# Three output parts together in the first block's second product, and a sparser chain of maxima

## The chip, the cores and the metric

The kernel runs on one core of a Trainium2 chip, as one launch. The metric is the device time of that launch in microseconds (us), the median of three runs. Engines are named PE (TensorE), DVE (VectorE), ACT (ScalarE), POOL (GpSimd) and SP (SyncE, which here only issues DMAs).

## The reference: what is computed

```python
# q, k, v: (4, 8, 768, 64): 4 batches, 8 heads, 768 tokens
k_sum = k.reshape(B, H, nb, 32, D).max(axis=3)      # 24 blocks of 32 keys
v_sum = v.reshape(B, H, nb, 32, D).mean(axis=3)
scores_l = scale * q @ k^T, kept where |i - j| < 16, else -1e9
scores_s = scale * q @ k_sum^T + log(32)
a = softmax(concat[scores_l, scores_s])             # sum + 1e-9
attn = a @ concat[v, v_sum]
# x = attn as (3072, 512); 4 experts, w1 (4, 512, 1024), w2 (4, 1024, 512)
p = domain_probs / (domain_probs.sum(-1) + 1e-9)
out = sum over e of p[:, e] * (relu(x @ w1[e]) @ w2[e])
```

All is float32. The kernel keeps the precision by splitting an operand into a high and a low part and adding three products of them.

## The kernel before, in words

**Tiling.** The 3072 tokens are 8 blocks of 384 (`TB`). A block's attention is 8 pieces (96 queries, 4 heads each). A piece loads keys and values, splits them on ACT and POOL (`stage_a`), makes scores on PE, maxima on DVE and exponentials on ACT (`scores`), normalises and splits the probabilities (`probs`), turns them by a DMA (`transposed`, tile awT), multiplies with the values on PE (`values`, tile px) and writes the block's x (`to_x`).

**The passes.** The first block is passed over alone with experts 0 and 1, the second alone with 1 and 0, then both together with 2 and 3. Blocks 2 to 7 go as three pairs with all four experts, in the order 2, 3, 1, 0 (`plan`, `pair_units`). A pass of one expert has a first product (tiles ph; in pairs pha, phb, phc, phd, by a scheme of seven products for eight) and a second one (tiles po, functions `second` and `mm2`). `mm2(tb, e, ts, hT, w2)` runs the output parts `ts` (a part is 128 tokens) through the eight chunks of w2: for each chunk and part three matmuls of 512 columns. So one part is 24 matmuls. It holds one bank of PSUM for each part from its first matmul until DVE has added the part to the sum (tile acc). There are four banks for ph and po (`ps_mm`), two for scores and two, `ps_av`, which px, the bank phd of pairs, and both tiles of the chain below share. `second` runs the last block of a pass as part 0 alone and then parts 1 and 2 together, before the change.

**The chain that spreads maxima.** In pairs the operands are 16 bit wide, after scaling by powers of two, found from the largest weights (tiles w0 to w3) and values (v1 to v3). `spread_maxima` brings a column of 128 maxima to one and back to all partitions, in four steps: 0, PE turns the column (tile w3t for expert 3); 1, DVE takes the maximum, limits and masks it and copies it out over 128 columns (tile w3e); 2, PE multiplies it with a piece of the identity (tile w3s); 3, DVE copies it back and `scales` works out factors (tile found). One call does at most one step. Steps wait on `passed`, a count of matmul time that the calling loops add up (2.1 us for a unit of a plain first product, 1.05 us for one of a pair's 28 products, 1.39 or 2.08 us for a unit of a second product). In a pair's first product the chain is only called after the 6th and the 7th of each seven products, so once or twice in 7.35 us. Seven chains run in all, one after another.

**What sets the order.** Instructions up to the first attention of block 0 are pinned to program order. Behind that a planner orders each engine's instructions by their place in the program and a timeline of its own; at run time every engine works through its list in order. Attention steps are put between units of the products, by the share of the pass that is done (`advance`). `prepare` scales the experts' weights on ACT and DVE, a step at a time; its 22nd, 42nd and 62nd steps are the first that need the factors of experts 3, 1 and 0.

Of the kernel before, what the change touches and what calls it, by code (L numbers as in the profile page):

```python
# [66 lines left out]
def attn_moe(ctx: ExitStack, tc: tile.TileContext, qvL, qv0, v0L, kD, kT, vT, w1L, w2L, dpL, cst, out):  # L67
# [60 lines left out]
    def facts(k):  # L128
        taken[0] += k
        return found[:, taken[0] - k : taken[0]]  # L130
# [9 lines left out]
    pending, last_matmul, passed = [], [None], [0.0]  # L140
    chain = dict(stage=0, due=0.0)

    def spread_maxima():

        if chain["stage"] == 0:
            if not pending:
                return
            chain["t"] = t = pending.pop(0)
            k = t["k"]
            t["turned"] = ps_av.tile([P, 512], F32, name=f"{t['name']}t", tag="av")[:k, 0:P]  # L150
            PE.transpose(t["turned"], t["m"], ident)
            chain.update(stage=1, due=passed[0] + 1.5)
            return
        if passed[0] < chain["due"]:
            return
        t = chain["t"]
        k = t["k"]
        if chain["stage"] == 1:
            most = facts(1)[:k]
            V.tensor_reduce(most, t["turned"], axis=AX.X, op=ALU.max)  # L160
            V.tensor_scalar(most, most, LEAST, MOST, op0=ALU.max, op1=ALU.min)
            bits = most.bitcast(I32)
            V.tensor_single_scalar(bits, bits, 0x7F800000, op=ALU.bitwise_and)
            t["every"] = sb.tile([P, P], F32, name=f"{t['name']}e", tag="hs", bufs=2)[:k]
            V.tensor_copy(t["every"], most.broadcast_to([k, P]))
            chain.update(stage=2, due=passed[0] + 3.0)
        elif chain["stage"] == 2:
            t["spread"] = ps_av.tile([P, 512], F32, name=f"{t['name']}s", tag="av")[:, 0:k]
            PE.matmul(t["spread"], t["every"], ident[:k, :k], start=True, stop=True)
            chain.update(stage=3, due=passed[0] + 1.5)  # L170
        else:
            V.tensor_copy(t["m"], t["spread"])
            t["then"](*scales(t["m"], k))
            chain["stage"] = 0

    def scales(m, k):

        both = facts(2 * k)
        s, inv = both[:, 0:k], both[:, k : 2 * k]
        V.tensor_scalar_mul(inv, m, 1.0 / TOP)  # L180
        V.tensor_scalar(s.bitcast(I32), m.bitcast(I32), -1.0, float(0x7F000000), op0=ALU.mult, op1=ALU.add)
        V.tensor_scalar_mul(s, s, TOP)
        return s, inv
# [855 lines left out]
    def mm2_halves(tb, e, t, hT, w2):  # L1039
        gt = tb * (TB // P) + t  # L1040
        pe = pw[:, gt, e : e + 1]
        for c in range(2):
            cols = slice(c * DM // 2, (c + 1) * DM // 2)
            po = ps_mm.tile([P, 512], F32, name=f"po{tb}_{e}_{t}{c}", tag="mm")[:, 0 : DM // 2]
            for m, (fc, (whi, wlo)) in enumerate(w2.items()):
                hh, hl = (x[:, t * P : (t + 1) * P] for x in hT[tb, fc])
                PE.matmul(po, hh, whi[:, cols], start=m == 0, stop=False)
                PE.matmul(po, hh, wlo[:, cols], start=False, stop=False)
                PE.matmul(po, hl, whi[:, cols], start=False, stop=m == FC - 1)
            V.scalar_tensor_tensor(acc[gt][:, cols], po, pe, acc[gt][:, cols], op0=ALU.mult, op1=ALU.add)  # L1050
            SP.dma_start(out[gt * P : (gt + 1) * P, cols], acc[gt][:, cols])
            yield 3 * FC * US2 / 2, 1.0

    def mm2(tb, e, ts, hT, w2):
        po = {t: ps_mm.tile([P, 512], F32, name=f"po{tb}_{e}_{t}", tag="mm") for t in ts}
        done = 0
        for m, (fc, (whi, wlo)) in enumerate(w2.items()):
            for t in ts:
                hh, hl = (x[:, t * P : (t + 1) * P] for x in hT[tb, fc])
                PE.matmul(po[t], hh, whi, start=m == 0, stop=False)  # L1060
                PE.matmul(po[t], hh, wlo, start=False, stop=False)
                last_matmul[0] = PE.matmul(po[t], hl, whi, start=False, stop=m == FC - 1)
                done += 3 * US2
            if m < FC - 1 and (len(ts) > 1 or m in (2, 5)):
                yield done, 1.0
                done = 0
        for t in ts:
            gt = tb * (TB // P) + t
            pe = pw[:, gt, e : e + 1]
            added[gt] = added.get(gt, 0) + 1  # L1070
            if added[gt] == 1:
                acc[gt] = sb.tile([P, DM], F32, name=f"acc{gt}", tag="acc", bufs=6)
                V.tensor_scalar_mul(acc[gt], po[t], pe)
            else:
                V.scalar_tensor_tensor(acc[gt], po[t], pe, acc[gt], op0=ALU.mult, op1=ALU.add)
            if added[gt] == E:
                SP.dma_start(out[gt * P : (gt + 1) * P, :], acc.pop(gt))
        yield done, 1.0
# [8 lines left out]
    def second(tbs, e, hT, w2, last):  # L1087
        whole = tbs if last else tbs[:-1]
        for tb in whole:
            for t in range(TB // P):  # L1090
                ends = last and (tb, t) == (tbs[-1], TB // P - 1)
                yield from mm2_halves(tb, e, t, hT, w2) if ends else mm2(tb, e, [t], hT, w2)
        for tb in tbs[len(whole) :]:
            yield from mm2(tb, e, [0], hT, w2)
            yield from mm2(tb, e, [1, 2], hT, w2)

    def with_steps(units, pr, e, w2):
        plain, final = pr is None, pr is not None and e == PAIRS[0][1][-1]
        if plain:
            steps = LATE if e == plan[2][1][-1] else ()  # L1100
        else:
            steps = SECOND if pr == SCALED else ()
        for n, us in enumerate(units):
            if plain and e in PLAIN:
                if 3 <= n < 3 + FC:
                    scan_w2(e, n - 3, w2[n - 3])
                if n == 3 + FC:
                    maxima_of(e)
                passed[0] += us[0]
                spread_maxima()  # L1110
            if not plain:
                passed[0] += us[0]
                spread_maxima()
                if pr == SCALED and n % 4 != 3:
                    next(looks.get(e, iter(())), None)
            if n in steps:
                next(preparing, None)
            if (pr, e) == FIRST7 and n in LAST2:
                next(preparing_last, None)
            soon = (12, 15) if (pr, e) in SEVENTH else (13, 17)  # L1120
            if final and pr < PAIRS[-1][0] and n in soon:
                fetch_parts(pr + 1, PAIRS[pr][1][0], soon.index(n))
            yield us

    def plain_units(tbs, e, early=0):
# [24 lines left out]
        for fc in order:  # L1150
            if fc not in w1:
                w1[fc] = weights(w1L, e, fc, "1", PL)
            for tb in tbs:
                us = mm1(fc, tb, w1[fc], KC // 2 if fc < early else 0)
                if e in PLAIN:
                    if tb == tbs[0]:
                        scan_plain(e, fc, w1[fc])
                    passed[0] += us[0]
                    spread_maxima()
                yield us  # L1160
            if fc not in w2:
                w2[fc] = weights(w2L, e, fc, "2", V if len(tbs) == 1 else PL)
        kept[e] = {fc: w1[fc] for fc in order[-4:]}, w2
        yield from with_steps(second(tbs, e, hT, w2, False), None, e, w2)


# [127 lines left out]
    def pair_units(pr, e, last=False):  # L1294
# [70 lines left out]
        if final:  # L1365
            yield from with_steps(seven_second(pr, tbs, e, hop), pr, e, {})
            return
        w2 = {fc: half2.pop((pr, e, fc)) for fc in range(FC)}
        yield from with_steps(second(tbs, e, hT, w2, last), pr, e, w2)


# [46 lines left out]
    for (tbs, experts), end in zip(plan, ENDS):  # L1418
# [11 lines left out]
        parts, due, u, done = None, [], 0.0, 0.0  # L1430
        for e, k in zip(experts, ease):
# [4 lines left out]
            for us, pace in units:  # L1436
# [4 lines left out]
                if nxt < NTB // 2 and u > whole - seconds[-1] + 1e-3:  # L1441
                    if parts is None:
                        xpair[nxt], parts = x_operands(nxt)
                    if due and u > due[0][0]:
                        due.pop(0)[1]()
                        due = [(max(t, u + XGAP), f) for t, f in due]
# [69 lines left out]
```

## Time and profile before

| | |
|---|---|
| three runs | 1138.64, 1131.49, 1139.86 us; median 1138.64 |
| the profiled execution | 1133.09 us, span 1131.3 us |
| granted TensorE clock, mean | 0.989 |
| PE / DVE / ACT / POOL busy | 1090.1 / 790.1 / 688.1 / 605.2 us |

The profiled execution has its own time beside its span: 1.8 us lie around the span. All rows below are of that execution, and times in them count from the span's start. A timeline row is start, duration, engine, line, operation, output <- inputs, count, and in brackets the idle time of the engine before it with what ended it. All engines' rows carry line 79, since one helper issues every instruction; tiles tell them apart.

### The profile page before, as it was taken

The page shows a single profiled execution, that of the slowest core. Times are in us where ns is not written, and L with a number is a line of the kernel's source. Part 1 is how long each engine was busy: PE and PEld are TensorE (multiplying, and loading weights), DVE is VectorE, ACT ScalarE, POOL GpSimd, SP SyncE. Part 2 cuts the span into 40 slices and gives each one's busy share as a digit, 9 for nine tenths or more (in the row PEclk, how much of TensorE's full clock was granted, in tenths as well). Part 3 has the DMA queues.
Part 4 walks back from the last instruction along what each step waited for, and adds up shares of the span by engine and source line. Part 5 has one row for each costly group of instructions (what it writes and reads, how often), then busy time and mean ns, then how long its engine had stood idle before and what let it go on. Part 6 is the DMA issues. An engine that isn't in the chain of part 4 may idle for free. (4 is left out here: it accounts for less than half of the span.)

```text
span 1131.3 us, 22766 instructions
## 1 busy us (share of the span) xinstructions
PE 1090.1 (96%) x7857; PEld 783.8 (69%) x7857; DVE 790.1 (70%) x1910; ACT 688.1 (61%) x1863; POOL 605.2 (53%) x722
## 2 busy tenths in 40 slices
PE   9898799999999899899999999999999999999998
PEld 7778688898898655555556455555586868686867
DVE  6668576568877986867888666666756875656573
ACT  5577476666597668777668455655636563636361
POOL 2298377785676645444274425444546664546451
PEclk9998989999999999999999999999999999999999
DMA  6598559667766788969899766564635482626201
GB/s 248 197 264 233 148 153 297 162 191 177 217 184 187 229 253 261 296 180 326 251 282 274 245 212 150 132 163 104 189 92 183 156 257 68 201 62 209 66 20 56
DMA packets 205027, 214.12 MB, mean 189 GB/s; under 512 B 82289, under 2 KB 140145, under 8 KB 204913
## 3 DMA queue, kind: packets, MB, share of 16 engines
q1 hardware_dynamic: 204912, 212.68, 64.3%
q8 instruction: 61, 1.00, 0.4%
q14 instruction: 54, 0.43, 0.1%
HBM read 157.45 MB, written 38.27 MB: 173 GB/s over the span
## 5 line engine op out<-in xcount | busy, mean ns | idle before, releaser
L79 POOL TENSOR_TENSOR ks<-kr,ks 128x304 fp32r<-128x304 f32 x112 | 101.4, 911 | 137.5 <-ACT ks L79 125.1
L79 PE MATMUL po<-w,hh 128*128 128x512 f32 x384 | 122.6, 399 | 0.0
L79 ACT ACTIVATE ms<-ms,nb 96x152 f32<-96x152 f32 x256 | 104.4, 415 | 19.0 <-DVE nb L79 18.4
L79 PE MATMUL po<-w2s,hh 128*128 128x512 f16 x384 | 114.8, 380 | 0.0
L79 PEld LDWEIGHTS <-wls 128*128 128x128 f16 x768 | 74.5, 98 | 48.7 <-issue 1.0
L79 PE MATMUL ph<-xh,wh 128*128 128x384 f32 x256 | 89.6, 354 | 9.1 <-ACT wh L79 5.6
L79 PEld LDWEIGHTS <-hh 128*128 128x128 f16 x576 | 53.3, 98 | 58.5
L79 PEld LDWEIGHTS <-hws 128*128 128x128 f16 x864 | 84.6, 98 | 13.2 <-issue 1.9
L79 POOL TENSOR_TENSOR wr2t<-wr2t 128x256 f32<-128x256 f32 x48 | 39.6, 829 | 98.9 <-PE phd L79 70.6
L79 DVE CUSTOM_DVE_ANT_0 ms<-psc,c_sb 96x152 f32<-96x152 f32 x256 | 68.7, 305 | 33.4 <-PE psc L79 32.3
L79 PE MATMUL ph<-xl,wh 128*128 128x384 f32 x256 | 88.1, 344 | 0.0
L79 PE MATMUL ph<-xh,wl 128*128 128x384 f32 x256 | 87.2, 343 | 0.1
L79 DVE TENSOR_TENSOR aw<-ms,aw 96x512 f16<-96x512 f32 x112 | 77.9, 728 | 11.2 <-ACT aw L79 9.7
L79 POOL TENSOR_TENSOR wl<-wr,wh 128x512 fp32r<-128x512 f32 x44 | 61.4, 1395 | 42.4 <-ACT wh L79 41.4
L79 PEld LDWEIGHTS po<-w,hh 128*128 128x128 f32 x384 | 70.8, 190 | 15.1
L79 PEld LDWEIGHTS <-wl 128*128 128x128 f16 x576 | 56.0, 98 | 35.7 <-issue 0.2
L79 ACT CAST aw<-ms 96x512 f16<-96x512 f32 x112 | 53.2, 522 | 42.1 <-issue 28.9
L79 POOL TENSOR_TENSOR qv<-qv,v 128x256 f32<-128x256 f32 x56 | 40.6, 736 | 70.7 <-ACT v L79 70.6
L79 PE MATMUL po<-w,hl 128*128 128x512 f32 x192 | 76.5, 400 | 0.0
L79 PE MATMUL phb<-x_t,wls 128*128 128x384 f16 x384 | 72.9, 326 | 0.3 <-ACT phb L79 0.2
L79 PE MATMUL pha<-x,wl 128*128 128x384 f16 x384 | 72.9, 326 | 0.0
L79 PE MATMUL po<-w2s,hl 128*128 128x512 f16 x192 | 72.5, 379 | 0.0
(226 smaller groups left out, 2934.9 us busy)
## 6 DMA issues: line engine op xcount, KB each, us to landing
qv<-in_qvL SPq DMA_DIRECT2D x56, 320.0 KB, 3.6
wls<-wd1s SPq DMA_DIRECT2D x64, 256.0 KB, 3.2
kr<-in_kD SPq DMA_DIRECT2D x56, 256.0 KB, 3.4
wr2t<-in_w2L SPq DMA_DIRECT2D x48, 256.0 KB, 2.8
wr<-in_w1L SPq DMA_DIRECT2D x44, 256.0 KB, 3.7
wr<-in_w2L SPq DMA_DIRECT2D x32, 256.0 KB, 3.5
wr2s<-in_w2L SPq DMA_DIRECT2D x32, 256.0 KB, 4.4
wr1s<-in_w1L SPq DMA_DIRECT2D x32, 256.0 KB, 4.1
```

The lines of the kernel that those rows point to most:

```text
L79: ins = getattr(self.engine, name)(*a, **kw)
```

## The change

The chain waits 4.0 of `passed` between the first call that sees a pending column and its step 0, then 2.5, 5.0 and 2.5 between steps, where it was nothing, 1.5, 3.0 and 1.5. In a pass over the first block alone (experts 0 and 1) the three parts run through w2 together; every other pass is as it was.

```diff
     def spread_maxima():
 
         if chain["stage"] == 0:
-            if not pending:
+            if not pending or passed[0] < pending[0].setdefault("due", passed[0] + 4.0):
                 return
...
             PE.transpose(t["turned"], t["m"], ident)
-            chain.update(stage=1, due=passed[0] + 1.5)
+            chain.update(stage=1, due=passed[0] + 2.5)
             return
...
             V.tensor_copy(t["every"], most.broadcast_to([k, P]))
-            chain.update(stage=2, due=passed[0] + 3.0)
+            chain.update(stage=2, due=passed[0] + 5.0)
...
             PE.matmul(t["spread"], t["every"], ident[:k, :k], start=True, stop=True)
-            chain.update(stage=3, due=passed[0] + 1.5)
+            chain.update(stage=3, due=passed[0] + 2.5)
...
         for tb in tbs[len(whole) :]:
-            yield from mm2(tb, e, [0], hT, w2)
-            yield from mm2(tb, e, [1, 2], hT, w2)
+            for ts in [(0, 1, 2)] if tbs == [0] else [(0,), (1, 2)]:
+                yield from mm2(tb, e, ts, hT, w2)
```

## Rows read from the trace of the kernel before

**Rows 1.** The page's first part: busy time, share of span and count of each engine.
```profile
PE 1090.1 (96%) x7857; PEld 783.8 (69%) x7857; DVE 790.1 (70%) x1910; ACT 688.1 (61%) x1863; POOL 605.2 (53%) x722
```
**Rows 2.** Waits of PE: who, for whom, us in total, times, longest.
```profile
PE px L79 <- DMA awT<-aw: 9.5, 3, 6.3
...
PE w3s L79 <- DVE w3e L79: 2.6, 1, 2.6
...
PE phd L79 <- DVE found L79: 1.6, 1, 1.6
...
PE w1s L79 <- DVE hl L79: 1.0, 1, 1.0
...
PE w0t L79 <- DVE found L79: 0.8, 1, 0.8
PE w0s L79 <- DVE hl L79: 0.8, 1, 0.8
...
PE w1t L79 <- DVE found L79: 0.4, 1, 0.4
```
**Rows 3.** Windows: length, then busy us of PE, PEld, DVE, ACT, POOL; granted clock, DMA.
```profile
113.00:141.00 28.00, 21.33 (x182) 16.74 (x180) 16.68 (x44) 11.90 (x41) 9.46 (x12) 0.95 0.58 150
...
1000.00:1100.00 100.00, 99.99 (x756) 73.71 (x754) 62.72 (x115) 47.29 (x101) 49.28 (x57) 1.00 0.31 94
```
**Rows 4.** PE's timeline around the two ends of the first block's passes.
```profile
84.68 0.33 PE L79 MATMUL ph<-xh,wh 128*128 128x384 f32 x1
...
132.17 0.63 PE L79 MATMUL po<-w,hh 128*128 128x512 f32 x2
132.63 0.39 PE L79 MATMUL po<-w,hl 128*128 128x512 f32 x1
139.28 0.61 PE L79 MATMUL px<-awT,v 128*64 128x96 f16 x10 [6.25 <-DMA awT<-aw]
```
**Rows 5.** DVE's timeline, the sums of po and what stands around them.
```profile
81.15 0.74 DVE L79 TENSOR_SCALAR acc<-po,pw 128x512 f32<-128x512 f32 x1
...
86.96 0.73 DVE L79 TENSOR_SCALAR acc<-po,pw 128x512 f32<-128x512 f32 x1
...
129.38 0.95 DVE L79 TENSOR_REDUCE ksr<-kch 128x24 f32<-128x768 f32 x1 [2.26 <-DMA kch<-in_kT]
...
134.36 1.42 DVE L79 TENSOR_TENSOR aw<-ms,aw 96x512 f16<-96x512 f32 x2
...
136.03 1.39 DVE L79 SCALAR_TENSOR_TENSOR acc<-po,pw,acc 128x512 f32<-128x512 f32 x2
141.34 0.95 DVE L79 TENSOR_REDUCE vsr<-vch 128x24 f32<-128x768 f32 x1 [3.92 <-DMA vch<-in_vT]
```
**Rows 6.** Tile po: durations min/median/max in ns, first and last start.
```profile
L79 PE MATMUL po<-w,hh x384: 387/392/628, 61.0 to 380.3; 128*128 128x512 f32 x192
```
**Rows 7.** PE's timeline behind the pass of expert 3 over blocks 0 and 1.
```profile
401.44 1.14 PE L79 MATMUL phb<-x_t,wss 128*128 128x384 f16 x6 [1.86 <-DVE phc L79]
```
**Rows 8.** Windows of the first pair, columns as in rows 3.
```profile
382.00:402.00 20.00, 15.16 (x137) 9.62 (x135) 18.95 (x52) 15.65 (x42) 11.93 (x15) 1.00 0.92 286
...
480.00:523.00 43.00, 43.00 (x307) 22.53 (x305) 27.18 (x66) 32.02 (x84) 18.31 (x23) 1.00 0.77 235
523.00:553.00 30.00, 25.15 (x157) 15.34 (x156) 27.64 (x71) 22.20 (x58) 13.51 (x17) 1.00 1.05 315
```
**Rows 9.** Windows around w1s, columns as in rows 3.
```profile
465.00:470.00 5.00, 2.41 (x13) 1.29 (x12) 5.00 (x9) 3.98 (x9) 2.40 (x4) 0.94 0.98 262
470.00:475.00 5.00, 5.00 (x23) 2.63 (x22) 4.28 (x15) 2.69 (x5) 1.85 (x3) 0.72 0.72 217
```
**Rows 10.** Tiles of the chain and users of its factors, as in rows 6.
```profile
L79 DVE COPY found<-v1s x1: 146/146/146, 317.7 to 317.7; 128x1 f32<-128x1 f32 x1
...
L79 DVE TENSOR_SCALAR xr<-xr,found x12: 603/612/1053, 356.6 to 905.4; 128x768 f32<-128x768 f32 x12
...
L79 DVE COPY found<-w1s x1: 144/144/144, 470.6 to 470.6; 128x2 f32<-128x2 f32 x1
```

## The prediction

> **What bounds the kernel now.** I read the page's engine line first: PE is busy 1090.1 of 1131.3 us, DVE is next with 790.1 [rows 1]. So the time is PE's work plus PE's idle time, and a change that removes no matmul can only move the second. The matmuls here stay the same in number and shape. Next the waits of PE [rows 2]: 9.5 us for turned probabilities (three waits, one of 6.3) and, which the edit aims at, six waits that belong to the chain of maxima: w3s 2.6, phd 1.6 (it waits for a bank that holds the turned column of w0 until DVE has reduced it), w1s 1.0, w0t 0.8, w0s 0.8, w1t 0.4. That is 2.6 + 1.6 + 1.0 + 0.8 + 0.8 + 0.4 = 7.2 us. Then the windows [rows 3]: at 1000 to 1100 us PE works 99.99 of 100, while at 113 to 141 us it works 21.33 of 28 and DVE, ACT and POOL are no fuller than 16.68; there a chain of dependences decides, and its last link is a DMA [rows 4].
>
> **Three parts together.** It touches experts 0 and 1 over the first block alone: 2 x 72 matmuls, the same ones in another order. The median of a matmul is 392 ns, its least 387, over 384 of them that run one part at a time or two parts in turn [rows 6], so going round three banks has no price that two would not show: I take 0 for the matmuls.
>
> What moves is DVE's sum of part 0 (0.74 us), from the middle of the pass to its end, beside the two others. Expert 0: the sums stood at 81.15, then two, of which the last ended at 86.96 + 0.73 = 87.7 [rows 5], while PE began the next first product at 84.68 [rows 4]. That product has the fourth bank at once; its second unit needs a sum done by about 84.68 + 2.1 = 86.8, the third by 88.9, the fourth by 91.0, at 2.1 us a unit. With a third sum the last ends at 87.7 + 0.74 = 88.4, before the fourth unit wants its bank. Between 0 and, if DVE takes a split of probabilities first (1.42 for two operations [rows 5]), some 1.4 us of wait; I take 0, as the last sum stood 3 us behind the end even with other work between.
>
> Expert 1: PE has run out of products at 133.0 and waits to 139.28 for the last turned probabilities of block 1 [rows 4]. These come from DVE's aw at 134.36, which was late itself because DVE, which works in order, stood 2.26 us for a load of keys before an unrelated reduction (129.38) [rows 5]. The sums of po stand behind aw, at 136.03. If the third sum stands there too it costs nothing, since PE has no product to run; if the planner puts all three ahead of aw, px comes 3 x 0.7 = 2.1 us later; if DVE gains by the sum that is gone from the middle, 0.7 earlier. I take 0 out of -0.7 to +2.1.
>
> So part one is worth nothing by itself. But the planner orders every engine's list anew behind it, and outside the chain's 7.2 us PE is idle for 1131.3 - 1090.1 - 7.2 = 34 us [rows 1, 2], 9.5 of them for awT. What is dealt there can come out several us either way, which goes into the range.
>
> **The chain.** No instruction is added and no DMA is moved: seven chains, each with one turn and one product on PE and some ten small operations on DVE, stand further apart. From the code, with units of 1.39 us at the end of a second product: w3's turn comes three units later, its DVE step two later, and its product (5.0 behind) falls out of the pass into the first pair's first product. That product has only calls behind the 6th and 7th of each seven, so every step there falls one round of 7.35 us later: w1 and w0, whose columns appear two units before the end of a second product, now are turned in the first round of the next first product, and end in the fourth and last round.
>
> What goes: w3s 2.6, w0t 0.8, w0's bank 1.6, w1t 0.4, together 5.4 us. w1s 1.0 and w0s 0.8 wait for hl, which reads phd, one of the two banks that the chain shares; in the next round the same reader stands there, so I leave them.
>
> What comes in their place. The three steps that newly fall into a first product of a pair (w3s, w1t, w0t) need a bank that phd uses too, and the nearest rows for that are just w1s and w0s: 1.0 and 0.8, so 0 to 3 x 1.0; I take 0.9 for each, 2.7, since both rows of this kind show it. And DVE is the one that is behind: it is busy 18.95 of 20 us at 382 to 402 and 27.64 of 30 at 523 to 553 [rows 8], so where PE no longer waits for w3e it waits a little later for phc, as it does already for 1.86 us at 401.44 [rows 7]. The free time of DVE, 1.05 and 2.36 us, is what PE can win in these two stretches without DVE's list being changed: 1.05 + 2.36 + w1t's 0.4 = 3.8 of the 5.4. By the new waits it is 5.4 - 2.7 = 2.7. These are the same lateness counted in two ways, so I don't add them; I take 2.5, with 0 (all given back) and 7.2 (all six waits gone) as ends.
>
> The clock: around w1s PE stands for 2.59 of 5 us, and the granted clock is 0.94 in that window and 0.72 in the next [rows 9]. A window of 5 us at the mean c has 10 x (1 - c) us at 1.2 instead of 2.4 GHz: 0.6 + 2.8 = 3.4 us, which cost 1.7 us. The stop at w1s I let stand, so 0, at most -1.7.
>
> Later factors: v1's chain ended at 317.7 and would end some 16 us later (the waits sum to 14 instead of 6, so 8 for itself and 8 for w2's chain before it), well ahead of its first user, xr at 356.6 [rows 10]; 0. For w1 and w0 the slack is small. w1's ended at 470.6 in the third round [rows 10], so now at about 478, in the fourth; the first scaling with it on ACT is the second unit of the second product, which by the code begins one unit of the round later. If ACT has to wait, what is queued behind it is exponentials and casts of the attention; PE's second product covers that, since its operands lie ready (PE is busy 43.00 of 43 us at 480 to 523 [rows 8]). 0, or up to two waits of 3 us if the cover is gone.
>
> **Sum.** Profiled execution 1133.1 - 0 - 2.5 = 1130.6. It lies 5.5 us under the median of the three runs, 1138.64; the four executions known (1131.5, 1133.1, 1138.6, 1139.9) have the mean 1135.8, which I take as the level of a median. 1135.8 - 2.5 = 1133.3, so 1133.
>
> **The rivals.**
> (a) Nothing comes back: DVE is the bound of the pairs' first products, and PE meets the same lateness at phc. For it: rows 8; against: at 480 to 523 DVE is busy 27.18 of 43, so the lateness has places to go. 1136.
> (b) All comes back and the new order does well: 7.2 + 1.7 for the clock, and half of the longest wait for awT, 3.1: 1135.8 - 12 = 1124. For it: the 6.3 us rest on one reduction that stood in the wrong place; against: no edit aims there.
> (c) Slower: the end of the first block's passes gets later. Place: px at 139.28. If the planner puts one more load-bound reduction ahead of aw, as the vsr one that waited 3.92 us and took 0.95 [rows 5], px comes 4.9 later, with the third sum ahead of it 5.6, and PE, at half clock while it starts again (0.95 in that window [rows 3]), loses about 1.7 more: +7.3 - 1 left of the chain's gain, 1142. It decides from the point where this outweighs 2.5 us, so with any such reduction. For it: it happened once already with kch; against: nothing in the edit asks for it.
> (d) Going round three banks lowers the clock. The rows speak against it: two parts in turn run at the same 387 to 392 ns [rows 6]. If PE fell to 1.2 GHz over both second products, 2 x 16.6 us (72 matmuls; two take from 132.17 to 132.63, so 0.23 us each [rows 4]) would double: 1136 - 3 + 33 = 1166. The Trainium skill, "TensorE: Matmul & The Clock Gate" (A second HAM failure mode: psum-queue depth-cycling), says that cycling through PSUM banks in each iteration leaves PE short idle moments and makes the clock oscillate; by that rule it would be this case, and the trace so far doesn't bear it out.
> (e) The change doesn't do what it says: the planner runs parts 1 and 2 between those of part 0 already, whenever part 0 lacks a chunk. Then part one is the order of before with another name; it is in the forecast's 0.
>
> **How the numbers follow.** Forecast, with what the new order deals at random (1128 to 1138): 0.50. (a) 0.15, (b) 0.20, (c) 0.14, (d) 0.01. The range goes from (b)'s far side to beyond (c): 1120 to 1145, with some 0.1 left at each end. A measurement of this kernel tells about 1% (11 us) from no change. Faster by over 1% takes (b) and the edge of the forecast: 0.20. Slower by over 1% takes (d) and the far part of (c): 0.10. The rest, 0.70, is within 1%.
>
> **What would show it.** In the profile after: PE's wait for w3e is gone or under 1 us; w0t and w1t wait, if at all, for hl and not for found; phd has no wait for found; a PE wait for phc near 400 us has grown by 1 to 2 us. The matmuls of po keep 387 to 392 ns. The three sums of expert 0 stand together behind its last matmul. Wrong would be: PE's idle time under 25 or over 45 us, a wait for awT that has changed by over 3 us (the new order then weighs more than the chain), or a half clock during po.

## The result, and the profile after

| | before | after |
|---|---|---|
| median of 7 runs each | 1134.61 us | 1122.51 us |
| lowest to highest | 1131.49 to 1139.86 | 1119.98 to 1127.77 |
| profiled execution, span | 1133.1, 1131.3 us | 1126.7, 1124.9 us |

The ratio is 0.9893, with a 95% interval from 0.9862 to 0.9925. So the change took 12 us off, where 2.5 were forecast; the time lies inside the range, where rival (b) had put it, outside the forecast's own 1128 to 1138, and the experiments below ask whether it got there by (b)'s mechanism.

The page's engine line of the kernel after, to stand beside [rows 1]:

```profile
PE 1092.3 (97%) x7857; PEld 785.9 (70%) x7857; DVE 791.7 (70%) x1910; ACT 687.5 (61%) x1863; POOL 604.0 (54%) x722
```

PE is as busy as before (2.2 us more), and the span is 6.4 us shorter: PE's idle time went from 41.2 to 32.6 us. Which waits went is told by the waits of PE of the kernel after:

```profile
PE phb L79 <- ACT phb L79: 5.1, 4, 2.5
PE px L79 <- DMA awT<-aw: 4.9, 2, 2.5
...
PE psc L79 <- DVE nb L79: 1.9, 1, 1.9
...
PE phb L79 <- DVE phc L79: 1.0, 3, 0.5
```

Against [rows 2] two things have changed. All six waits of the chain of maxima are gone, w3s, phd for found, w1s, w0t, w0s and w1t, 7.2 us. And the waits for turned probabilities have gone from 9.5 to 4.9 us, the longest from 6.3 to 2.5. New or grown are phb for ACT's phb, with 2.5 us in one place, and psc (scores) for nb (the maxima of scores on DVE) with 1.9.

The windows of [rows 3], [rows 8] and [rows 9], now of the kernel after:

```profile
113.00:141.00 28.00, 25.15 (x197) 19.93 (x196) 18.77 (x49) 13.60 (x48) 11.90 (x16) 0.94 0.68 169
382.00:402.00 20.00, 19.99 (x140) 12.36 (x140) 17.39 (x46) 16.71 (x42) 12.59 (x16) 0.91 0.95 277
450.00:460.00 10.00, 8.53 (x44) 4.76 (x45) 7.77 (x23) 8.73 (x27) 7.79 (x11) 0.83 1.11 307
465.00:470.00 5.00, 5.00 (x34) 3.13 (x31) 4.10 (x9) 3.12 (x7) 3.83 (x4) 1.00 0.93 323
470.00:475.00 5.00, 5.00 (x33) 3.11 (x33) 5.00 (x19) 4.58 (x13) 1.58 (x1) 1.00 0.74 232
```

At 113 to 141 us PE works 25.15 of 28 us where it worked 21.33, and at 382 to 402 us 19.99 of 20 where it worked 15.16. The clock at 465 to 475 us is 1.00, where it was 0.94 and 0.72. But at 382 to 402 us it is now 0.91, where it was 1.00, and at 450 to 460 us there is a stretch at a low clock as well.

To see what a stage gained one needs windows that hold the same work on both sides, not the same times. So I cut at the start of the last po matmul of two passes: expert 0 over the first block, and expert 1 over the second. First the kernel before:

```profile
84.40:187.00 102.60, 91.20 (x633) 78.62 (x633) 73.02 (x177) 63.96 (x193) 69.11 (x76) 0.92 0.70 194
187.00:1131.30 944.30, 922.27 (x6715) 641.46 (x6713) 663.60 (x1553) 571.52 (x1528) 495.77 (x588) 1.00 0.63 185
```

and the kernel after:

```profile
87.00:181.30 94.30, 88.90 (x634) 77.73 (x634) 70.06 (x178) 63.24 (x191) 69.57 (x74) 0.93 0.76 208
181.30:1124.90 943.60, 924.25 (x6715) 642.02 (x6713) 666.78 (x1553) 572.00 (x1531) 495.37 (x591) 1.00 0.64 185
```

The first stretch, which holds the passes of expert 1 over either block, shrank from 102.60 to 94.30 us, by 8.3 us. The matmuls in it are as many (633 and 634 records). Idle time fell from 102.60 - 91.20 = 11.40 to 94.30 - 88.90 = 5.40, so by 6.0 us; the other 2.3 are busy time, of which the granted clock explains 1.6 at most (by the rounded clocks 2 x 0.08 x 102.6 = 16 us at half clock before, 2 x 0.07 x 94.3 = 13 after; PE stood still in a part of them, which costs no busy time). What the rest is stays open. The second stretch, with the other passes, all pairs and all seven chains in it, went from 944.30 to 943.60: idle time 2.7 us less, busy time 2.0 us more. In front of both stands the start, 84.4 us before and 87.0 after. Together 2.6 - 8.3 - 0.7 = -6.4, the difference of the spans. That the medians are 12.1 apart is not against this: the profiled execution of before lay 1.5 us under its median, that of after 4.2 above its own. The length of the start swings from run to run, with no relation to the edits that these profiles can tell: in the eight profiles here of kernels with the three parts of expert 0 together it had 82.0 to 88.5 us, mean 85.7, in the six without 82.1 to 86.8, mean 84.6.

Where the 6 us of idle time were, the timelines show. Most of it, 3.85 us, is the stop at the end of expert 1's pass. PE of the kernel after, to stand beside [rows 4]:

```profile
134.53 0.39 PE L79 MATMUL po<-w,hl 128*128 128x512 f32 x1
137.32 0.44 PE L79 MATMUL px<-awT,v 128*64 128x96 f16 x10 [2.40 <-DMA awT<-aw]
```

The pass ends at 134.53 + 0.39 = 134.92 and px begins at 137.32, 2.40 us later; before it was 6.25. DVE of the kernel after, to stand beside [rows 5]:

```profile
129.17 0.17 DVE L79 TENSOR_SCALAR rs<-rs 96x4 f32<-96x4 f32 x1 [1.07 <-ACT ms L79]
...
129.58 0.79 DVE L79 TENSOR_TENSOR ms<-ms,rs 96x608 f32<-96x608 f32 x1
131.09 1.94 DVE L79 TENSOR_REDUCE ksr<-kch 128x24 f32<-128x768 f32 x2 [0.73 <-DMA kch<-in_kT]
132.95 0.95 DVE L79 TENSOR_TENSOR aw<-ms,aw 96x512 f16<-96x512 f32 x2
```

The normalise (rs, ms) now stands ahead of the reductions of keys that wait for their load (ksr), of which two stand between ms and aw and wait 0.73 us together. Before, a reduction that had waited 2.26 us for its load stood ahead of rs, and between ms at 131.43 and aw at 134.36 one more that waited 1.28. DVE of the kernel before, two rows that [rows 5] leaves out:

```profile
130.25 0.15 DVE L79 TENSOR_SCALAR rs<-rs 96x4 f32<-96x4 f32 x1
...
133.49 0.95 DVE L79 TENSOR_REDUCE ksr<-kch 128x24 f32<-128x768 f32 x1 [1.28 <-DMA kch<-in_kT]
```

SP's queue shows the result. Kernel before:

```profile
135.87 1.32 SPq L79 DMA_TRANSPOSE awT<-aw  x1
```

Kernel after:

```profile
133.97 1.28 SPq L79 DMA_TRANSPOSE awT<-aw  x1
```

These are the last transposes of block 1's probabilities. From their issue to px it is the same time in both, 139.28 - 135.87 = 3.41 and 137.32 - 133.97 = 3.35 us. So the wait at px is set by where aw's end, and with it that issue, stands against the end of the pass: 2.85 us behind it before, 0.95 ahead of it after.

The rest of the 6 us is 0.45 at the px of the piece before (2.99 us before, 2.54 after) and a second stop, of 1.69 us, that is gone. It stood in the next first product, where PE wants the bank of an earlier product that DVE has still to read for hl, the low part of that product's result. PE of the kernel before, and DVE ahead of it:

```profile
155.15 0.52 PE L79 MATMUL ph<-xh,wh 128*128 128x384 f32 x1 [1.69 <-DVE hl L79]
```

```profile
152.34 1.26 DVE L79 TENSOR_SCALAR rs<-rs 96x4 f32<-96x4 f32 x1 [2.99 <-ACT ms L79]
...
154.55 1.48 DVE L79 SCALAR_TENSOR_TENSOR hl<-ph,hh 128x384 fp32r<-128x384 f32 x3
```

Three hl stood there behind a normalise that had waited 2.99 us for ACT. In the kernel after, three hl stand ahead of that normalise (at 147.75, 149.32 and 151.34, the normalise at 152.96), and PE doesn't wait. So this stop, too, is a matter of place on DVE.

### The profile page after: what moved, and what is told of

Same layout as the page of the kernel before. It is cut to its first block, busy times and chain, and to the rows that moved or that the text cites. A ratio compares the mean times of both kernels' runs of the same rounds, so it can differ in the third digit from the quotient of the medians.

```text
span 1124.9 us, 22751 instructions
## 1 busy us (share of the span) xinstructions
PE 1092.3 (97%) x7857; PEld 785.9 (70%) x7857; DVE 791.7 (70%) x1910; ACT 687.5 (61%) x1863; POOL 604.0 (54%) x722
## 4 chain that ended last, share of the span: by engine, by line
PE 49%; DVE 9%; ACT 6%; DMA 5%; POOL 4%; issue 2%; SPq 0%; POOLq 0%; ACTq 0%; DVEq 0%
PE po L79 13%; PE phb L79 8%; PE pob L79 5%; PE pha L79 5%; PE poa L79 3%; PE phc L79 3%; PE phd L79 3%; PE ph L79 2%; PE poc L79 2%; DMA qv<-in_qvL 2%; PE pod L79 1%; PE px L79 1%; POOL wr2t L79 1%; PE psc L79 1%; ACT hws L79 1%
## 5 line engine op out<-in xcount | busy, mean ns | idle before, releaser
L79 DVE TENSOR_TENSOR aw<-ms,aw 96x512 f16<-96x512 f32 x112 | 75.1, 700 | 12.6 <-ACT aw L79 10.9
```

Source lines behind the costliest of these rows:

```text
L79: ins = getattr(self.engine, name)(*a, **kw)
```

## Experiments

All ratios are to the kernel before on the same chip, with 95% intervals; each experiment was timed in five rounds. "Two passes" is the first stretch above, cut in the same way in each profile, "rest" what follows to the end of the span; both are of one profiled execution, which can lie some us off the median (that of e9 lay 4.9 us above its own). The table is for looking back to.

| kernel | ratio | two passes, us | rest, us |
|---|---|---|---|
| before | 1 | 102.6 | 944.3 |
| after | 0.9893 [0.9862, 0.9925] | 94.3 | 943.6 |
| e1 three parts, both experts | 0.9909 [0.9886, 0.9931] | 92.2 | 947.7 |
| e2 chain alone | 0.9971 [0.9953, 0.9988] | 102.4 | 941.4 |
| e3 three parts, expert 0 | 0.9886 [0.9864, 0.9907] | 94.2 | 943.5 |
| e4 three parts, expert 1 | 1.0011 [0.9994, 1.0028] | 103.3 | 942.7 |
| e5 keys later, parts as before | 0.9939 [0.9920, 0.9959] | 97.8 | 941.8 |
| e9 e3, keys earlier | 0.9954 [0.9933, 0.9975] | 98.0 | 949.2 |
| e12 e3, keys later | 0.9894 [0.9857, 0.9932] | 93.3 | 946.5 |
| e6 e3 and the chain | 0.9883 [0.9861, 0.9906] | 93.5 | 944.1 |
| e7 e3, only the start's delay | 0.9938 [0.9917, 0.9959] | 93.4 | 947.8 |
| e8 e3, only the gaps | 0.9898 [0.9868, 0.9928] | 92.2 | 945.9 |
| e10 only the gaps | 0.9990 [0.9970, 1.0010] | 104.0 | 948.3 |
| e11 only the start's delay | 1.0016 [0.9996, 1.0035] | 103.0 | 949.6 |

**The two edits apart (e1, e2).** e1 has the second hunk of the change only, e2 the first only.

```diff
 e1
-            yield from mm2(tb, e, [0], hT, w2)
-            yield from mm2(tb, e, [1, 2], hT, w2)
+            for ts in [(0, 1, 2)] if tbs == [0] else [(0,), (1, 2)]:
+                yield from mm2(tb, e, ts, hT, w2)
 e2
-            if not pending:
+            if not pending or passed[0] < pending[0].setdefault("due", passed[0] + 4.0):
...
-            chain.update(stage=1, due=passed[0] + 1.5)
+            chain.update(stage=1, due=passed[0] + 2.5)
...
-            chain.update(stage=2, due=passed[0] + 3.0)
+            chain.update(stage=2, due=passed[0] + 5.0)
...
-            chain.update(stage=3, due=passed[0] + 1.5)
+            chain.update(stage=3, due=passed[0] + 2.5)
```

> The kernel before with only the three parts together in the first block's passes; the chain as before. Theory (the two edits add up; this one works through the order at the end of the first block's passes): the profile of after shows 7.7 us less from the end of expert 1 over block 0 to the end of expert 1 over block 1, and 0.7 less before that, so -8 us: about 1126 where before is at 1134.6. PE's last wait for awT before block 1 near 2.4 us instead of 6.3, and the chain's waits (w3s, w0t, w1s) still there. Rival (the gain needs both edits, or is the chain's): within 3 us of before.

> The kernel before with only the sparser chain; parts as before. Theory: -2 to -4 us (the profile of after has 2.4 us less over the first pair), so 1131 to 1133; PE's wait for awT at 139 us as before, 6.3 us, and none for w3e. Rival (the chain carries the gain): -8 us or more. Rival (DVE is the bound there and nothing comes back): within 1 us.

Measured: e1 1125.26 us, 0.9909; e2 1132.83 us, 0.9971. The three parts alone bring some 10 us, the chain alone 3. In e1 the longest wait for awT is 2.53 us and the chain's waits are all still there; in e2 it is 6.28 and they are gone but for 0.2 us at w1s. So the gain that was forecast at 0 is the large one, and it sits in the two passes: 92.2 us against 102.6.

**Which expert's pass (e3, e4).** Three parts together for one expert alone; e4 has `e == 1` in place of `e == 0`.

```diff
-            yield from mm2(tb, e, [0], hT, w2)
-            yield from mm2(tb, e, [1, 2], hT, w2)
+            for ts in [(0, 1, 2)] if tbs == [0] and e == 0 else [(0,), (1, 2)]:
+                yield from mm2(tb, e, ts, hT, w2)
```

> Three parts together for expert 0 alone; expert 1 over block 0 and the chain as before. In DVE's list the normalising and splitting of the last piece of block 1 now stand ahead of the last key reduction, as in after. Theory (it is that place in DVE's list): nearly all of the gain of the three parts, -6 to -8 us, 1127 to 1129, awT wait under 4 us. Rival (it is the work at the end of expert 1's pass itself, its sums and its order of parts): like before, awT wait above 5 us.

> Three parts together for expert 1 over block 0 alone; expert 0 and the chain as before. In DVE's list all four key reductions stand ahead of the last piece's split, as in before, and a sum of po besides. Theory (place in DVE's list): no gain, 1133 to 1136, awT wait 6 us or more. Rival (the end of expert 1's pass itself): -6 to -8 us, 1127 to 1129.

Measured: e3 1122.42 us, 0.9886; e4 1136.52 us, 1.0011. All of the gain comes from expert 0's pass, though the stop that goes is at the end of expert 1's. In e4 the place where PE stops has the three parts together, and nothing is won. DVE's timeline of e4 ahead of the stop:

```profile
130.98 0.95 DVE L79 TENSOR_REDUCE ksr<-kch 128x24 f32<-128x768 f32 x1 [1.90 <-DMA kch<-in_kT]
131.85 0.16 DVE L79 TENSOR_SCALAR rs<-rs 96x4 f32<-96x4 f32 x1
...
135.22 0.95 DVE L79 TENSOR_REDUCE ksr<-kch 128x24 f32<-128x768 f32 x1 [0.75 <-DMA kch<-in_kT]
136.09 1.42 DVE L79 TENSOR_TENSOR aw<-ms,aw 96x512 f16<-96x512 f32 x2
```

and PE's stop:

```profile
140.99 0.61 PE L79 MATMUL px<-awT,v 128*64 128x96 f16 x10 [6.01 <-DMA awT<-aw]
```

That is the order of before: a reduction that waited 1.90 us for its load ahead of rs, another (0.75) ahead of aw, and px waits 6.01 us. The same stage of e3, DVE:

```profile
123.17 0.17 DVE L79 TENSOR_SCALAR rs<-rs 96x4 f32<-96x4 f32 x1 [1.07 <-ACT ms L79]
...
124.52 0.95 DVE L79 TENSOR_REDUCE ksr<-kch 128x24 f32<-128x768 f32 x1 [0.97 <-DMA kch<-in_kT]
...
126.95 0.95 DVE L79 TENSOR_TENSOR aw<-ms,aw 96x512 f16<-96x512 f32 x2
```

PE:

```profile
131.31 0.40 PE L79 MATMUL px<-awT,v 128*64 128x96 f16 x10 [2.39 <-DMA awT<-aw]
```

Its last three parts of expert 1 are apart as before, but rs stands ahead of the reduction that waits, and aw ends at 126.95 + 0.95 = 127.90; px waits 2.39. The window of e3's two passes:

```profile
82.00:176.20 94.20, 87.63 (x634) 76.51 (x633) 70.85 (x178) 63.48 (x193) 70.28 (x74) 0.95 0.78 210
```

The idle time of the two passes is 94.20 - 87.63 = 6.57 us, and busy time is 3.6 us under before's 91.20. By the clocks 0.92 and 0.95 some 16 and 9 us were at half clock, so up to 3.5 of the 3.6 us is that: with the shorter stops went less time at half clock. How much of it PE paid in busy time the mean clock can't say: e9 below has 0.91 and a busy time of 88.78.

**The order on DVE by another edit (e5), and taken back (e9).** If the place of the key reductions (ksr) is what counts, moving them alone should do part of it. e5 is the kernel before with only the reductions of the second batch's keys (`b == 1`, blocks 2 and 3; `take_k`, which sends the maxima on as well) due 0.6 later in the plan, their loads as before; e9 is e3 with them due 0.2 earlier (the same line with `- 0.2`).

```diff
-                    (k0 + dk * hp + lead, lambda b, hp=hp, take=take: take(b, hp), b),
+                    (k0 + dk * hp + lead + (0.6 if b == 1 and take is take_k else 0.0), lambda b, hp=hp, take=take: take(b, hp), b),
```

> The kernel before, with both edits away; only the key reductions of block 1's batch stand 0.6 of a piece later in the program. In DVE's list the last piece's normalising and splitting now stand ahead of the last reduction, much as in after. Theory (place in DVE's list): awT wait under 4 us, no wait for hl at 155, -6 to -9 us, 1126 to 1129. Rival (three parts are needed for it): like before within 2 us.

> Three parts together for expert 0 alone, with the key reductions of that batch 0.2 of a piece earlier, which puts all of them ahead of the last piece's split, as in before. Theory (place in DVE's list): the gain goes again, awT wait 5 us or more, 1132 to 1136. Rival (three parts help by themselves): stays at 1122 to 1125.

Measured: e5 1128.64 us, 0.9939; e9 1129.98 us, 0.9954. DVE of e5 at the end of expert 1's pass:

```profile
127.91 0.17 DVE L79 RECIPROCAL rs<-rs 96x4 f32<-96x4 f32 x1
129.81 0.95 DVE L79 TENSOR_REDUCE ksr<-kch 128x24 f32<-128x768 f32 x1 [1.73 <-DMA kch<-in_kT]
...
132.24 0.68 DVE L79 TENSOR_TENSOR aw<-ms,aw 96x512 f16<-96x512 f32 x1
...
133.50 0.34 DVE L79 TENSOR_TENSOR aw<-ms,aw 96x192 f16<-96x192 f32 x1
```

and PE:

```profile
137.26 0.61 PE L79 MATMUL px<-awT,v 128*64 128x96 f16 x10 [4.50 <-DMA awT<-aw]
```

The normalise's small steps stand ahead of the waiting reduction again, aw ends at 133.84 and px waits 4.50; the stop for hl at 155 us is gone too. The parts run as in before, so three parts together are not needed for this gain; half of it came by moving the keys. In e9 the three parts of expert 0 are together, and DVE has the order of before:

```profile
127.42 0.95 DVE L79 TENSOR_REDUCE ksr<-kch 128x24 f32<-128x768 f32 x1 [1.85 <-DMA kch<-in_kT]
128.29 0.16 DVE L79 TENSOR_SCALAR rs<-rs 96x4 f32<-96x4 f32 x1
...
131.91 0.95 DVE L79 TENSOR_REDUCE ksr<-kch 128x24 f32<-128x768 f32 x1 [1.66 <-DMA kch<-in_kT]
132.78 1.42 DVE L79 TENSOR_TENSOR aw<-ms,aw 96x512 f16<-96x512 f32 x2
```

1.85 us of waiting for a load ahead of rs, 1.66 ahead of aw. PE of e9:

```profile
137.74 0.79 PE L79 MATMUL psc<-ks,qs 128*96 128x152 f32 x2 [6.08 <-ACT ks L79]
139.04 0.61 PE L79 MATMUL px<-awT,v 128*64 128x96 f16 x10 [0.51 <-DMA awT<-aw]
```

The stop is as long as before's, 6.08 + 0.51 us, and more than half of the gain in time is gone. But this stop doesn't hang on DVE's order alone. The list of PE has scores (psc) ahead of px there, which wait for split keys (ks), and SP had four transfers of key maxima to issue ahead of the transpose. SP's queue of e9:

```profile
132.90 2.61 SPq L79 DMA_DIRECT2D ks<-ksr  x4
135.60 1.34 SPq L79 DMA_TRANSPOSE awT<-aw  x1
```

aw ended at 132.78 + 1.42 = 134.20, 2.54 us behind the end of the pass at 131.66; the transpose went out 1.40 us after that. So reductions due 0.2 earlier changed three lists, and e9 doesn't test DVE's alone. It also keeps a part of the gain: its two passes are 98.0 us, not 102.6, and it has no stop for hl.

What the order on DVE is worth is told best by all profiles together. In before, e2, e4, e10 and e11 a reduction that waits stands ahead of rs, PE has the stop for hl (1.3 to 1.8 us), and the two passes take 102.4 to 104.0 us. In after, e1, e3, e6, e7, e8 and e12 rs stands ahead, there is no stop for hl, and they take 92.2 to 94.3. e5, which shares no line with the change, moves the reductions alone and gets about half: 97.8 us, ratio 0.9939. So that the place of these reductions carries about half of the gain, with the parts apart, is shown by e5; that the order on DVE carries the rest, in the kernels with three parts together, is read from the traces.

**Does the chain add to it (e6)?** e3 and the whole chain edit (the diffs of e3 and e2).

> Three parts together for expert 0 alone, and the sparser chain. Theory (the two add up): 1122.4 - 2.8 = 1119.6. Rival (the chain's gain is one way out of many of the new order of the pairs): 1122 to 1126.

Measured: 1122.05 us, 0.9883; e3 had 0.9886. The two do not add up: the chain's 3 us of e2 are not there on top of e3, and from e1 to the kernel after it is 0.9909 to 0.9893. So the chain is worth 3, 2 and 0 us beside three different orders; only the first is told from nothing by its interval.

**The halves of the chain edit (e7, e8, e10, e11).** The start's delay alone, and the gaps alone, on e3 (e7, e8) and on the kernel before (e11, e10): of e2's diff the first hunk, or the other three.

> Three parts together for expert 0 alone; of the chain only the delay of 4.0 before its first step, the gaps as before. Theory (w0t, w1t and the bank of w0 go by the start, w3s by start and gaps): w0t and w1t don't wait for found any more, 1120 to 1122 beside 1122.4 without. Rival (the gaps do it): 1122 to 1123 with the waits in other places.

> Three parts together for expert 0, and of the chain only the longer gaps (2.5, 5.0, 2.5), with no delay at its start. Theory A (the chain's waits are lateness that each new order of the pairs deals anew; the gaps themselves are worth little): the waits for w3e and for found are gone, about 5 us of them, but others of 2 to 3 us appear, and the time is within 3 us either side of three parts for expert 0 alone (ratio 0.985 to 0.992 against the kernel before). Theory B (the gaps carry the gain and the start delay alone spoils it): 3 to 6 us under three parts for expert 0 alone, ratio 0.983 or less.

> The kernel before with only the longer gaps of the chain, no delay at its start, parts as before. Theory B (gaps carry the gain): ratio 0.994 to 0.998, as the whole chain edit alone had (0.9971) or better. Theory A (dealt anew): ratio anywhere from 0.996 to 1.004, with the waits for w3e and found gone and waits for phb or psc in their place. In both the wait for awT of about 6 us stays, since the chain first runs long behind it.

> The kernel before with only the delay of 4.0 at the chain's start, gaps and parts as before. Beside three parts for expert 0 this delay cost some 6 us. If that is the delay's own price: ratio 1.004 to 1.007 here. If it was what that one order of the pairs dealt: anywhere between 0.998 and 1.004 here, and the waits that appear stand at other places than there.

Measured: e7 1129.43 us, 0.9938; e8 1125.85 us, 0.9898; e10 1134.96 us, 0.9990; e11 1138.42 us, 1.0016. The start's delay alone costs some 6 us beside e3 and 1.8 (interval -0.5 to 4.0) beside the kernel before; the gaps alone cost 1.4 us and -1.1, neither told from nothing. I had expected the gaps alone to take w3s and found away; they do not: e8 and e10 keep w3s at 2.5 us and phd for found at 1.6 and 1.5. So neither half carries the gain of e2 by itself, and theory B, that the gaps do, falls. With the start's delay the turns and found's readers move on, w1s and w0s are gone from the waits, and a stop for scores comes in their stage: in e11 psc waits 3.28 us for nb at 463.14, in e7 3.34 us at 455.27. With both halves w3s is gone as well, and what stands there then is another stop: in e2 phb waits 2.52 us for ACT's phb at 390.38. The kernel after has both kinds. Its PE behind the pass of expert 3 over blocks 0 and 1, and in the first pair:

```profile
382.01 1.14 PE L79 MATMUL phb<-x_t,wss 128*128 128x384 f16 x6 [2.52 <-ACT phb L79]
...
451.21 0.62 PE L79 MATMUL psc<-ks,qs 128*96 128x152 f32 x4 [1.87 <-DVE nb L79]
```

These 2.52 us stand in the unit where w3s had its 2.6, and each of the two is followed by a stretch at half clock (0.91 over 382 to 402 us is 3.6 us of it, and 0.83 over 450 to 460 us is 3.4), where before only w1s was. So the second stretch gained 2.7 us of idle time and lost 2.0 of busy time. Over all kernels here the rest is 941.4, 943.6 and 944.1 us with the whole chain edit, 941.8 to 949.2 us in the seven without any of it, and 945.9 to 949.6 in the four with a half. So it differs by up to 8 us from profile to profile, and the chain's own 2 or 3 are inside that. How much of the 8 is the new order on DVE, ACT and POOL and how much is one execution against another (those of before alone spread from 1130 to 1141 us) the profiles don't tell apart.

**Both edits for the first stretch (e12).** e3 with e5's line.

> Three parts together for expert 0, and the keys of batch 1 due 0.6 later as well. With the first edit one reduction of keys still stands between the last piece's normalise and its split; this takes it behind the split. If the reduction there still costs PE time, the wait for awT falls from about 2.4 to 1.2 to 2.0 us and the time is 1 to 2 us under three parts for expert 0 alone (ratio 0.985 to 0.988). If the two edits do the same thing and the rest is the DMA's own time, the time is that of three parts for expert 0 alone, 0.9886 within 0.002. If their effects added up, it would be 0.9886 x 0.9939 = 0.9826.

Measured: 1125.39 us, 0.9894, two passes 93.3 us, the longest wait for awT 2.9. The two gains do not add up (that would be 0.9826), and e3's time is not beaten. The edit did not do all that I wanted, though: in e12's list a reduction that waited 1.32 us (at 131.06) still stands between ms and aw, so what px would gain without it stays untested. No kernel here is told from the kernel after by its interval in the direction of faster; e3, which needs the one line for expert 0 and no change of the chain, is as fast.

## Why the prediction was right or wrong

**The bound** was read rightly: PE's work stayed (1090.1 and 1092.3 us), and all that moved was idle time and clock. **The matmuls of po** too. Tile po of the kernel after, to stand beside [rows 6]:

```profile
L79 PE MATMUL po<-w,hh x384: 388/392/500, 64.7 to 375.3; 128*128 128x512 f32 x192
```

388 and 392 ns against 387 and 392: going round three banks has no price, and rival (d) did not come. From 66.0 to 87.4 us and from 114.0 to 134.9 us, where the three parts run, PE works all of the time and the granted clock is 1.00. So the rule of the Trainium skill cited there ("TensorE: Matmul & The Clock Gate", A second HAM failure mode: psum-queue depth-cycling), that going through PSUM banks in each iteration leaves short idle moments and a clock that swings, is not borne out here.

**Part one taken as 0: this is the step that failed.** Its single costs were right. The three sums of expert 0 stand behind its pass and nothing waits for them:

```profile
86.10 0.75 DVE L79 TENSOR_SCALAR acc<-po,pw 128x512 f32<-128x512 f32 x1 [0.35 <-PE po L79]
...
87.48 0.74 DVE L79 TENSOR_SCALAR acc<-po,pw 128x512 f32<-128x512 f32 x1
...
88.94 0.74 DVE L79 TENSOR_SCALAR acc<-po,pw 128x512 f32<-128x512 f32 x1
```

(DVE, kernel after; the next pass's first product begins at 87.28.) What failed is "I take 0 out of -0.7 to +2.1" for the end of expert 1's pass, and "part one is worth nothing by itself". I asked where the third sum would go in DVE's list and held the rest of that list fixed; so this term reached 0.7 us to the good side, and the wait at px alone gave 3.85, the two passes 8.3. I did write that the planner deals every list anew, but put that into the range as chance, with no place and no price. That the measured time lies in the range is owed to this allowance and to (b), not to the forecast's sum. The list was not fixed, and the code said so: `mm2` yields three times for part 0 alone and eight times for parts 1 and 2 together, eleven units to this second product; for three parts together it yields eight times. The attention's steps are dealt between units. So expert 0's pass gives other places to them, and the planner puts what follows elsewhere. That it is expert 0's pass is shown by e3 and e4, and that the place on DVE of the key reductions moves px by e5 and the rows of both kernels; that the count of units is what moved the steps is read from the code and not tried by itself.

**Rival (b)** had the right place and a good size: "half of the longest wait for awT, 3.1" came as 3.85, and 1124 stands against 1122.5. Its sentence against, "no edit aims there", was no argument: a stop that hangs on one instruction's place in a list goes or stays with any edit that redoes the list. But (b) put more of its 12 us down to the chain, 7.2 + 1.7, and there it was wrong: the chain's waits went, yet others took 4.5 of the 7.2 us of idle time, and 2.0 of what was left went into busy time, most of it half clock. That its sum came so near was luck: by the windows the chain's part is 0.7 us of the profile's 6.4, and the two passes are 8.3.

**The chain at -2.5**, between 0 and 7.2: the size was right for the chain alone (0.9971 of 1135.67 is 3.3 us, with 1.4 to 5.3 as ends), but it is not a term to add: on e3 it is 0. Of its signs w3e gone, w0t and w1t gone and phd no longer waiting for found came as said. Wrong was where the lateness would show. I said phc near 400 us, 1 to 2 us more; the waits for phc are now 0.5 at the longest, and it shows at phb for ACT's phb and at psc. Wrong too was "the stop at w1s I let stand": w1s no longer waits at all, and the 3.4 us of half clock there went.

**The signs of being wrong**: a wait for awT changed by over 3 us was named as the sign that the new order weighs more than the chain. It changed by 3.8, and it does. **Rival (a)** fell with the time. **(c)** had the right place, the key reductions ahead of aw, with the other sign; in e9 an edit of 0.2 in the plan puts the reductions back ahead of aw. **(e)** fell too, as part one moved the time by 10 us.

## What to carry to other kernels

Where a planner or a hand-written list interleaves two streams, an edit that changes how many units a loop yields is an edit of the whole order behind it; look for the longest stop that rests on one instruction's place in an in-order engine's list, and price that stop going or staying, whatever the edit aims at. A reduction that waits for a load belongs behind the work that another engine is about to wait for: here the end of aw against the end of the pass, plus 3.4 us for the transpose, gave the wait within 0.1 us in before, after, e3, e4 and e5; in e9, where other transfers stood ahead of the transpose, it was 1.4 us longer. And waits removed in a stretch where another engine is nearly full are to be counted by what the stretch gains between equal work, not by the rows that vanish: here 7.2 us of rows gave 2.7 of idle time and 0.7 of time in one profile on each side, and 3.3 us in e2, the chain alone.

## What the hardware showed that I had not expected

The same stop did not cost the same clock. In the kernel before, e1 and e3 PE has the same two waits there, 1.54 or 1.55 us for phd and, one us of work later, 1.05 or 1.04 at w1s for hl: 2.59, 2.59 and 2.58 us together. Two windows of e1 (457 to 467 us; the first begins within the wait for phd):

```profile
457.00:462.00 5.00, 2.60 (x12) 1.43 (x12) 5.00 (x12) 3.96 (x10) 2.37 (x4) 0.82 1.05 271
462.00:467.00 5.00, 5.00 (x17) 2.41 (x16) 3.81 (x12) 2.13 (x4) 1.14 (x2) 0.50 0.63 213
```

and the same of e3:

```profile
457.00:462.00 5.00, 3.02 (x18) 1.79 (x18) 5.00 (x14) 3.83 (x9) 2.29 (x5) 1.00 0.93 238
462.00:467.00 5.00, 5.00 (x34) 3.20 (x33) 4.37 (x13) 2.98 (x7) 0.71 (x1) 1.00 0.76 259
```

By the granted clock that is 1.8 + 5.0 = 6.8 us at 1.2 GHz in e1, none in e3, and 3.4 in the kernel before. So one stop of this length cost 0, 1.7 or 3.4 us beside its own time, and the prediction's "at most -1.7" was read from one of the outcomes. The other kernels that keep this pair of waits fall into the same classes: e4, e5, e8 and e12 have a granted clock of 1.00 around it, e9 has 6.8 us at 1.2 GHz (0.66 over 466 to 476 us). What decides between them the runs do not show.
